# Block sums of w2 made mid-run and parked in DRAM, seven-product chunks from 9 to 15 with a plain last chunk, output rows together

## The chip, the cores and the metric

One core of a Trainium2 chip runs the whole program. The metric is the device time of one execution in microseconds (us). TensorE (PE) does the matmuls, VectorE (DVE), ScalarE (ACT) and GpSimd (POOL) the elementwise work; all DMAs are issued by SyncE (SP), in order, from one hardware queue.

## The reference

Attention over 8 batches and 8 heads of width 64: 512 local rows attend to the 65 nearest local rows and 32 global ones, 32 global rows attend to all. Its output x (8 x 544 x 512) goes through a two-dimensional Fourier transform and a feed-forward layer:

```python
X = np.fft.fft(x, axis=1)
X = np.fft.fft(X, axis=2)
u = x + np.real(X)
un = (u - mean(u)) / np.sqrt(var(u) + 1e-06)
return u + np.maximum(un @ w_ch1, 0.0) @ w_ch2     # w_ch1 512 x 2048, w_ch2 2048 x 512
```

The weights come as float64. All products keep float32 accuracy by splitting each factor into a float16 high and low part and summing three of the four partial products.

## The kernel before

**Stages.** The weights are loaded and split (names `w_...`). The attention runs over 32 head pairs (`load`, `scores`, `masked`, `exps`, `p_hi`, `p_lo`, `turn`, `values`, `norm`, and `g_...` for the global rows); `turn` is a DMA transpose. The Fourier stage of a batch (`d_...`) begins when its four pairs are done. The feed-forward layer (`l_...`, `f_...`) runs over 17 chunks of 256 rows: chunk 2b+k is half k of batch b, and chunk 16 holds the 32 rows that each batch has left over. So chunks, Fourier stages and attention of later batches overlap on the engines.

**A chunk.** For each of 8 pieces fp of the hidden width (256 columns), `f_first` (L1189) makes the first product in PSUM (`ps1`), `f_hi` (L1198, ACT) and `f_lo` (L1202, DVE) make the two halves of its ReLU, and `f_second` multiplies by w2. The plain form (L1211, chunks 0 to 9) is 2 x 6 matmuls of 512 columns for one fp. Chunks 10 to 16 (`c >= FAST`) use a seven-product (Strassen-Winograd) form, `f_fast` (L1263): 21 matmuls of 256 columns for one fp. It needs sums of the blocks of the ReLU (`f_relu` L1216 on ACT, `f_mix` L1221 to L1224 on DVE, `f_mhi` L1232 on ACT, `f_mlo` L1236 on POOL), and at the chunk's end `f_copy` and `f_join` (L1267 to L1279), before the residual `f_end` (L1284, DVE, one for each half j of 128 rows) and the store `f_out` (L1290; L1293 for chunk 16). During a chunk of that form the PSUM tile S (tag A) holds partial sums.

**The sums of w2.** That form also needs sums of the blocks of w2, hi and lo, one set `tw` for each fp: `t_sum` (L1150) adds hi and lo of the weights, `t_mix` (L1157 to L1160) makes four block sums, both on DVE, `t_hi` (L1171, ACT) and `t_lo` (L1176, DVE) split them. All operands lie in SBUF. The scratch tiles are those of the attention (`ph`, `pe`), and the sets are kept in its input buffers (`THOME`: qk, kT, vf, vN, vS). So the tasks wait for `done`: the last `scores` and `turn` and the last `g_turn`.

**The order.** `Plan.order` is a list scheduler that runs when the program is built: every task has an engine, an estimated duration, predecessors, buffers and a due time, and the plan fixes the order of each engine's instructions, SP's queue included. At the same time the task with the lower class goes first, then the earlier due time. The table `REL` gives earliest start times and `BIAS` shifts due times, by kind of task and stage. On the chip each engine then works through its list in that order, and waits wherever the next task's inputs aren't there.

The store of chunk 16 takes the rows to four batches for each half:

```python
for j in range(2):
    nc.sync.dma_start(self.out[4 * j:4 * j + 4, SL:T, :], u[:, j])
```

Of the kernel before, what the change touches and what calls it, by code (L numbers as in the profile page):

```python
# [32 lines left out]
FAST = 10  # L33
# [1575 lines left out]
```

## Time and profile before

| | us |
|---|---|
| median of 3 runs (1004.98, 1006.74, 1006.92) | 1006.74 |
| the profiled execution, its own time | 1002.04 |
| its span, first to last instruction | 1000.3 |
| PE busy | 890.2 |
| DVE busy | 654.8 |
| ACT busy | 614.5 |
| POOL busy | 630.3 |

The span's sum is made against the profiled execution; 1.74 us of its time lie outside the span, and the median of the runs is 4.70 us above it. Busy time is that of instructions on the engine, as the profile models their ends. A row of the timeline gives start, duration, engine, line and tile names, and in brackets the idle time ahead of it with what ended it.

### The profile page before, as it was taken

The page shows a single profiled execution, that of the slowest core. Times are in us where ns is not written, and L with a number is a line of the kernel's source. Part 1 is how long each engine was busy: PE and PEld are TensorE (multiplying, and loading weights), DVE is VectorE, ACT ScalarE, POOL GpSimd, SP SyncE. Part 2 cuts the span into 40 slices and gives each one's busy share as a digit, 9 for nine tenths or more (in the row PEclk, how much of TensorE's full clock was granted, in tenths as well). Part 3 has the DMA queues.
Part 4 walks back from the last instruction along what each step waited for, and adds up shares of the span by engine and source line. Part 5 has one row for each costly group of instructions (what it writes and reads, how often), then busy time and mean ns, then how long its engine had stood idle before and what let it go on. Part 6 is the DMA issues. An engine that isn't in the chain of part 4 may idle for free.

```text
span 1000.3 us, 31158 instructions
## 1 busy us (share of the span) xinstructions
PE 890.2 (89%) x12589; PEld 678.0 (68%) x12589; DVE 654.8 (65%) x1946; ACT 614.5 (61%) x1305; POOL 630.3 (63%) x905
## 2 busy tenths in 40 slices
PE   2652449999999999999999999996999999999993
PEld 1442337667676757667676766664889988888883
DVE  5987986257655676477556757599785755854442
ACT  6897788957786768697587766333443433443331
POOL 5599777796889688689959999217343432441211
PEclk8555559999999999999999999998999999999998
DMA  9998966558899667879779665620221311111000
GB/s 315 315 272 276 313 143 131 158 102 177 170 194 216 183 128 129 181 174 191 175 149 214 124 137 116 125 91 1 69 32 35 70 22 44 32 36 44 1 23 21
DMA packets 213785, 133.20 MB, mean 133 GB/s; under 512 B 165792, under 2 KB 183296, under 8 KB 213640
## 3 DMA queue, kind: packets, MB, share of 16 engines
q1 hardware_dynamic: 213640, 131.21, 56.0%
q8 instruction: 98, 1.61, 0.7%
q14 instruction: 47, 0.39, 0.1%
HBM read 64.98 MB, written 18.35 MB: 83 GB/s over the span
## 4 chain that ended last, share of the span: by engine, by line
PE 76%; DVE 11%; ACT 3%; DMA 3%; issue 2%; POOL 2%; SPq 1%; POOLq 0%; DVEq 0%; ACTq 0%
PE ps L1189 33%; PE acc L1211 19%; PE acc L1263 7%; PE S L1263 5%; PE bk L729 3%; PE S L681 2%; DVE tw L1176 1%; PE S L671 1%; PE bk L732 1%; DMA rw<-in_moe_w_ch 1%; DVE tf L1150 1%; DMA pl<-ph 1%; PE psd L1031 1%; PE S L764 1%; PE psd L998 1%
## 5 line engine op out<-in xcount | busy, mean ns | idle before, releaser
L1189 PE MATMUL ps<-uh,wh 128*128 128x256 f16 x3264 | 383.4, 274 | 0.7 <-DVE h L1202 0.7
L1189 PEld LDWEIGHTS <-wh 128*128 128x128 f16 x3264 | 315.4, 98 | 48.7 <-issue 1.5
L1211 PE MATMUL acc<-wh,h 128*128 128x512 f16 x960 | 224.4, 380 | 2.5 <-DVE h L1202 2.5
L1236 POOL TENSOR_TENSOR hs<-fz,hs 128x512 f16<-128x512 f32 x56 | 65.8, 1176 | 178.5 <-ACT hs L1232 132.4
L1211 PEld LDWEIGHTS <-h 128*128 128x128 f16 x960 | 88.7, 98 | 97.6 <-DVE h L1202 3.5
L1202 DVE SCALAR_TENSOR_TENSOR h<-ps,h 128x512 f16<-128x512 f32 x113 | 77.5, 686 | 58.6 <-ACT h L1198 58.2
L1198 ACT ACTIVATE h<-ps 128x512 f16<-128x512 f32 x113 | 66.9, 593 | 63.2 <-PE ps L1189 60.2
L1216 ACT ACTIVATE fx<-ps 128x512 f32<-128x512 f32 x56 | 33.4, 597 | 103.6 <-PE ps L1189 103.6
L700 ACT ACTIVATE pe<-pe,nm 128x160 f32<-128x160 f32 x256 | 87.8, 414 | 12.1 <-DVE nm L691 12.1
L707 POOL TENSOR_TENSOR ph<-pe,ph 128x512 f16<-128x512 f32 x64 | 76.7, 1198 | 28.3 <-ACT ph L703 27.5
L691 DVE CUSTOM_DVE_ANT_0 pe<-S,msk,z 128x160 f32<-128x160 f32 x192 | 62.2, 379 | 37.7 <-PE S L681 27.1
L1221 DVE TENSOR_TENSOR fz<-fx 128x128 f32<-128x128 f32 x56 | 20.5, 366 | 88.7 <-ACT fx L1216 87.5
L1263 PEld LDWEIGHTS <-hs 128*128 128x128 f16 x672 | 65.4, 98 | 8.5 <-POOL hs L1236 1.0
L1232 ACT ACTIVATE hs<-fz 128x512 f16<-128x512 f32 x56 | 35.3, 630 | 45.0 <-DVE fz L1224 43.5
L729 PEld LDWEIGHTS <-pl 128*64 128x64 f16 x1536 | 45.3, 117 | 23.1 <-issue 16.3
L729 PE MATMUL bk<-vN,pl 128*64 128x65 f16 x768 | 52.2, 203 | 8.5 <-DVE x L743 4.9
L621 POOL TENSOR_TENSOR vN<-vf,vN 128x640 f16<-128x640 f32 x32 | 43.3, 1356 | 14.0 <-ACT vN L617 10.6
L729 PE MATMUL bk<-vS,pl 128*64 128x65 f16 x768 | 51.7, 203 | 0.5 <-DMA vS<-vN 0.5
L732 PE MATMUL bk<-vN,pl 128*64 128x65 f16 x1024 | 48.9, 202 | 0.0
L703 ACT ACTIVATE ph<-pe 128x640 f16<-128x640 f32 x64 | 46.3, 726 | 1.8 <-DMA pl<-ph 1.0
L1263 PE MATMUL acc<-tw,hs 128*128 128x256 f16 x336 | 46.2, 273 | 0.4 <-POOL hs L1236 0.4
L506 POOL TENSOR_TENSOR wh<-wm,wh 128x512 f16<-128x512 f32 x32 | 36.9, 1159 | 11.9 <-ACT wm L499 10.5
(246 smaller groups left out, 1977.0 us busy)
## 6 DMA issues: line engine op xcount, KB each, us to landing
qk<-in_qk SPq DMA_DIRECT2D x32, 512.0 KB
vf<-in_v SPq DMA_DIRECT2D x32, 320.0 KB
raw<-in_moe_w_ch SPq DMA_DIRECT2D x17, 512.0 KB
vS<-vN SPq DMA_DIRECT2D x64, 130.0 KB
xs<-x SPq DMA_DIRECT2D x32, 256.0 KB
out<-u SPq DMA_DIRECT2D x16, 512.0 KB
x<-xs SPq DMA_DIRECT2D x24, 256.0 KB
u<-xs SPq DMA_DIRECT2D x24, 256.0 KB
```

Source lines behind the costliest of these rows:

```text
L691: nc.vector.tensor_tensor_reduce(self.per[(4 * p + j) % 4][:, h], S[:, h, 160 * n:160 * n + 160], self.msk[:, j], z[:, 8:9], 3e38, op0=ALU ...
L700: nc.scalar.activation(pe[:, h], pe[:, h], AF.Exp, bias=nm[:, n, h:h + 1], scale=-1.0)
L703: self.nc.scalar.activation(self.phr[i % 2][:, :, 96:256], self.pe2[i % 2], AF.Copy)
L707: self.nc.gpsimd.tensor_sub(ph[:, :, 256:384], pe[:, :, 32:160], ph[:, :, 128:256])
L729: nc.tensor.matmul(pv[r, n, h], pl[:, 3 * h + 1 + a, r], v, start=x == 0, stop=False)
L732: nc.tensor.matmul(pv[r, n, h], pl[:, 3 * h, r], vN[:, 4, c, h], start=False, stop=c == 1)
L1189: nc.tensor.matmul(ps[:, q], wt[:, w, c0:c0 + P], uh[:, :, 4 * a + kt, :], start=n == 0, stop=n == 11)
L1198: self.nc.scalar.activation(h[:, 0], self.fps[c, fp], AF.Relu)
L1202: self.nc.vector.scalar_tensor_tensor(h[:, 1], self.fps[c, fp], 0.0, h[:, 0], op0=ALU.max, op1=ALU.subtract)
L1211: nc.tensor.matmul(self.acc_f[c, j], h[:, a, q, j * P:(j + 1) * P], self.w[1, f][:, w, :], start=f == 0 and a == 0 and w == 0, stop=f == 1 ...
L1236: self.nc.gpsimd.tensor_sub(h[:, 1], self.fz.pop((c, fp)), h[:, 0])
L1263: nc.tensor.matmul(o, l[x], r[y], start=bool(first) and fp == 0 and n == 0, stop=bool(last) and fp == 7 and n == 2)
```

## The change

- `FAST, LAST = 9, 16` and `fast(c)`: the seven-product form is used for chunks 9 to 15. Chunk 16 is plain, without `f_copy` and `f_join`.
- The sums of w2 have scratch tiles of the Fourier stage (`x4` for the four sums, `eh` for the halves). They wait only for the weights, not for the attention; REL holds the unit of these tasks back to 235.6 in the plan's time. A new task `t_out` stores each set (512 KB) in a DRAM tile `td`, and `t_in` loads it into the place in SBUF where `t_hi` and `t_lo` put it before, after `done` (fp 4 to 7 also after the last `values` and `g_values`). The three sets with two places load by two DMAs: 8 stores, 11 loads.
- `f_hi` of chunk 9, all eight, and its first `f_relu` wait for `done`; its `f_second` for `t_in` of the same fp.
- The output tensor has 8 x 544 rows in the order in which the chunks make them, and the host puts them in place. Chunk 16 stores each half of 128 adjacent rows with a DMA of its own right after its `f_end` (`f_last`).
- The plan's estimates of the t tasks grow (1.2, 1.5, 1.2, 1.2 to 1.4, 1.9, 1.25, 1.6).
- `REL` and `BIAS` have other values. Apart from the loads of the weights, these are those of batches 2 and later, of chunks from 2 on, of the units T and f; attention and Fourier stages of batches 0 and 1 keep theirs.

```diff
-FAST = 10
+FAST, LAST = 9, 16
...
+def fast(c):
+    return FAST <= c < LAST
...
+        self.td = [dr.tile([P, 2, 2, 2, 256], F16, name=f"td{f}") for f in range(8)]
...
     def t_sum(self, fp):
-        f = self.cp.tile([P, 2, 512], F32, name="tf", tag="ph")
+        f = self.p1.tile([P, 4, 512], F32, name="tf", tag="x4")
...
+    def t_out(self, fp):
+        self.nc.sync.dma_start(self.td[fp], self.te.pop(fp))
+
+    def t_in(self, fp):
         home = THOME[fp]
         if len(home) == 2:
             t = [self.cp.tile([P, 2, 2, 256], F16, name="tw", tag=h) for h in home]
+            for i in range(2):
+                self.nc.sync.dma_start(t[i], self.td[fp][:, i])
         else:
             t = self.cp.tile([P, 2, 2, 2, 256], F16, name="tw", tag=home[0])
+            self.nc.sync.dma_start(t, self.td[fp])
...
     def f_out(self, c):
...
-        if b < B:
-            nc.sync.dma_start(self.out[b, 256 * k:256 * k + 256, :].rearrange("(j p) c -> p j c", j=2), u)
-        else:
-            for j in range(2):
-                nc.sync.dma_start(self.out[4 * j:4 * j + 4, SL:T, :], u[:, j])
+        self.nc.sync.dma_start(self.out[256 * c:256 * c + 256, :].rearrange("(j p) c -> p j c", j=2), self.u.pop(c))
+
+    def f_last(self, c, j):
+        self.nc.sync.dma_start(self.out[256 * c + P * j:256 * c + P * j + P, :], self.u[c][:, j])
...
-            add(("t_sum", fp), DVE, 1.2, self.t_sum, fp, after=done, seq=[("t_sum", fp - 1)] if fp else [], new=tf)
-            add(("t_mix", fp), DVE, 1.5, self.t_mix, fp, after=[("t_sum", fp)], seq=[("t_mix", fp - 1)] if fp else [], use=tf, new=tm)
...
+            add(("t_sum", fp), DVE, 1.4, self.t_sum, fp, after=[("w_lo", 16 + 2 * fp), ("w_lo", 17 + 2 * fp)], seq=[("t_sum", fp - 1)] if fp else [], new=[tf])
+            add(("t_mix", fp), DVE, 1.9, self.t_mix, fp, after=[("t_sum", fp)], use=[tf])
+            add(("t_hi", fp), ACT, 1.25, self.t_hi, fp, after=[("t_mix", fp)], seq=[("t_hi", fp - 1)] if fp else [], use=[tf], new=[te])
+            add(("t_lo", fp), DVE, 1.6, self.t_lo, fp, after=[("t_hi", fp)], use=[tf, te])
+            add(("t_out", fp), SP, .5, self.t_out, fp, after=[("t_lo", fp)], use=[te], kb=512)
+            add(("t_in", fp), SP, .6, self.t_in, fp, after=[("t_out", fp)] + done + ([("values", 63), ("g_values", 15)] if fp > 3 else []), seq=[("t_in", fp - 1)] if fp else [], new=tw, kb=512)
...
+            if c == 16:
+                for j in range(2):
+                    add(("f_last", c, j), SP, .6, self.f_last, c, j, after=[("f_end", c, j)], use=[u], kb=256, due=T + 20)
+                continue
...
-_OUT = (8, T, DM)
+_OUT = (8 * T, DM)
```

## Rows read from the trace of the kernel before

**Rows 1.** The page: the span, and the busy tenths of PE in 40 equal slices.

```profile
span 1000.3 us, 31158 instructions
...
PE   2652449999999999999999999996999999999993
```

**Rows 2.** Stretches: length, busy of PE, PEld, DVE, ACT, POOL (instructions), PE clock, DMA share, GB/s.

```profile
100.00:150.00 50.00, 23.17 (x341) 18.32 (x339) 44.79 (x118) 40.73 (x90) 38.83 (x61) 0.59 0.85 228
200.00:640.00 440.00, 437.82 (x7352) 305.38 (x7351) 276.85 (x934) 316.49 (x716) 361.15 (x537) 1.00 0.76 161
675.00:703.00 28.00, 19.20 (x150) 14.25 (x148) 27.77 (x34) 10.83 (x19) 18.36 (x18) 0.88 0.00 1
```

**Rows 3.** Waits of PE from 195 to 990 us: total, times, longest.

```profile
PE psd L998 <- DVE z L1020: 7.7, 1, 7.7
PE acc L1211 <- DVE h L1202: 2.5, 2, 2.2
...
PE ps L1189 <- DVE h L1202: 0.7, 1, 0.7
```

**Rows 4.** DVE, 674 to 688 us: start us, us, engine, line, operation, tiles, count.

```profile
674.05 5.87 DVE L1176 TENSOR_TENSOR tw<-tm,tw 128x512 f16<-128x512 f32 x2
...
687.07 0.46 DVE L1020 SCALAR_TENSOR_TENSOR z<-psd,z 128x274 f16<-128x274 f32 x1
```

**Rows 5.** Timeline of POOL, 674 us.

```profile
674.28 2.34 POOL L901 TENSOR_TENSOR s<-x 128x1020 f32<-128x1020 f32 x1
```

**Rows 6.** Timeline of PE, 648 to 706 us.

```profile
648.46 1.46 PE L1211 MATMUL acc<-wh,h 128*128 128x512 f16 x6
...
689.38 3.37 PE L1211 MATMUL acc<-wh,h 128*128 128x512 f16 x12
...
703.11 2.75 PE L1211 MATMUL acc<-wh,h 128*128 128x512 f16 x12
705.70 1.47 PE L1189 MATMUL ps<-uh,wh 128*128 128x256 f16 x12
```

**Rows 7.** Instructions on tile tw and tf: duration ns min/median/max, first and last start.

```profile
L1150 DVE TENSOR_TENSOR tf<-wh x16: 675/684/1207, 644.5 to 695.3; 128x512 f32<-128x512 f16 x16
L1157 DVE TENSOR_TENSOR tm<-tf x8: 415/420/947, 646.4 to 698.0; 128x256 f32<-128x256 f32 x8
...
L1176 DVE TENSOR_TENSOR tw<-tm,tw x16: 673/686/3119, 650.5 to 702.3; 128x512 f16<-128x512 f32 x16
```

**Rows 8.** Groups of DVE by line, 200 to 640 us: busy us, mean ns.

```profile
L1107 DVE TENSOR_TENSOR unh<-un,unh 128x512 f16<-128x512 f32 x18 | 15.2, 846 | 1.1 <-ACT unh L1103 1.1
```

**Rows 9.** Timeline of SP, the last transpose of the attention.

```profile
636.60 1.52 SPq L713 DMA_TRANSPOSE pl<-ph  x1
```

**Rows 10.** Timeline of all engines, 980 to 1000.3 us.

```profile
980.76 1.47 PE L1189 MATMUL ps<-uh,wh 128*128 128x256 f16 x12
...
982.83 0.59 ACT L1198 ACTIVATE hx<-ps 128x512 f16<-128x512 f32 x1
...
983.97 0.68 DVE L1202 SCALAR_TENSOR_TENSOR hx<-ps,hx 128x512 f16<-128x512 f32 x1
...
986.84 0.49 PE L1263 MATMUL S<-wh,hs 128*128 128x256 f16 x3
...
989.55 1.42 DVE L1284 SCALAR_TENSOR_TENSOR u<-fy,ve,u 128x512 f32<-128x512 f32 x2
990.33 1.27 SPq L1293 DMA_DIRECT2D out<-u  x2
```

**Rows 11.** DMA from 987 to 1000.3 us, 40 slices of 0.33 us, and packets.

```profile
GB/s 0 0 0 0 0 0 0 0 0 0 0 0 0 6 55 12 18 6 25 55 68 68 105 105 92 99 105 105 105 105 99 99 99 86 55 6 0 0 0 0
DMA packets 264, 0.52 MB, mean 39 GB/s; under 512 B 8, under 2 KB 8, under 8 KB 264
```

**Rows 12.** The same from 911 to 920 us, 40 slices of 0.225 us.

```profile
GB/s 0 0 0 0 0 0 0 0 0 0 0 0 0 0 0 246 400 400 355 410 391 128 0 0 0 73 0 0 0 0 0 0 0 0 0 0 0 0 0 0
DMA packets 273, 0.54 MB, mean 60 GB/s; under 512 B 16, under 2 KB 16, under 8 KB 272
```

More of the change, by code (lines that the diff above doesn't have):

```diff
@@ L1152, in t_mix, with t_lo @@
     def t_mix(self, fp):
-        ve, f = self.nc.vector, self.tf.pop(fp)
-        t = [self.cp.tile([P, 2, 256], F32, name="tm", tag=f"pe{i}") for i in range(2)]
-        self.tm[fp] = t
+        ve, f = self.nc.vector, self.tf[fp]
+        t = f[:, 2:4].rearrange("p a (b n) -> p (a b) n", b=2)
         (b11, b12), (b21, b22) = ((f[:, q, 0:256], f[:, q, 256:512]) for q in range(2))
-        ve.tensor_sub(t[0][:, 0], b12, b11)
-        ve.tensor_sub(t[0][:, 1], b22, t[0][:, 0])
-        ve.tensor_sub(t[1][:, 0], b22, b12)
-        ve.tensor_sub(t[1][:, 1], t[0][:, 1], b21)
+        ve.tensor_sub(t[:, 0], b12, b11)
+        ve.tensor_sub(t[:, 1], b22, t[:, 0])
+        ve.tensor_sub(t[:, 2], b22, b12)
+        ve.tensor_sub(t[:, 3], t[:, 1], b21)
     def t_hi(self, fp):
+        self.te[fp] = t = self.p1.tile([P, 2, 2, 2, 256], F16, name="te", tag="eh")
+        for i in range(2):
+            self.nc.scalar.activation(t[:, i, 0].rearrange("p a n -> p (a n)"), self.tf[fp][:, 2 + i], AF.Copy)
+    def t_lo(self, fp):
+        f, t = self.tf.pop(fp), self.te[fp]
+        for i in range(2):
+            self.nc.vector.tensor_sub(t[:, i, 1].rearrange("p a n -> p (a n)"), f[:, 2 + i], t[:, i, 0].rearrange("p a n -> p (a n)"))
+    def t_out(self, fp):
+        self.nc.sync.dma_start(self.td[fp], self.te.pop(fp))
+    def t_in(self, fp):
         home = THOME[fp]
@@ L1489, in run @@
             add(("d_rest", b), SP, 1.0, self.d_rest, b, after=[("d_addp", b, 2), ("d_addv", b, 2)], use=[("xfm", b)], kb=64, **kr)
+        done = [(n, i) for n in ("scores", "turn") for i in (62, 63)] + [("g_turn", 15)]
         for fp in range(8):
-            done = [(n, i) for n in ("scores", "turn") for i in (62, 63)] + [("g_turn", 15)]
-            tf, tm, tw = [("ph", "t", fp, x) for x in range(2)], [("per", "t", fp, x) for x in range(4)], [(h, "t", fp, x) for x, h in enumerate(TFREE[fp])]
-            add(("t_sum", fp), DVE, 1.2, self.t_sum, fp, after=done, seq=[("t_sum", fp - 1)] if fp else [], new=tf)
-            add(("t_mix", fp), DVE, 1.5, self.t_mix, fp, after=[("t_sum", fp)], seq=[("t_mix", fp - 1)] if fp else [], use=tf, new=tm)
-            add(("t_hi", fp), ACT, 1.2, self.t_hi, fp, after=[("t_mix", fp)] + ([("values", 63), ("g_values", 15)] if fp > 3 else []), seq=[("t_hi", fp - 1)] if fp else [], use=tm, new=tw)
-            add(("t_lo", fp), DVE, 1.2, self.t_lo, fp, after=[("t_hi", fp)], use=tm)
+            tf, te, tw = ("x4", "t", fp), ("eh", "t", fp), [(h, "t", fp, x) for x, h in enumerate(TFREE[fp])]
+            add(("t_sum", fp), DVE, 1.4, self.t_sum, fp, after=[("w_lo", 16 + 2 * fp), ("w_lo", 17 + 2 * fp)], seq=[("t_sum", fp - 1)] if fp else [], new=[tf])
[4 more added lines that the diff above has]
+            add(("t_in", fp), SP, .6, self.t_in, fp, after=[("t_out", fp)] + done + ([("values", 63), ("g_values", 15)] if fp > 3 else []), seq=[("t_in", fp - 1)] if fp else [], new=tw, kb=512)
         add(("l_load",), SP, .8, self.l_load, after=[("d_rest", b) for b in range(B)] + [("load_pair", 7, 1)], new=[("u", 16)], kb=512)
@@ L1528, in run @@
                         use=[uh] + ([ps] if q else []), new=[] if q else [ps], cls=8, due=T, alts=[["ps1"], ["bank"]] if c > FAST and q == 0 else None)
-                add(("f_hi", c, fp), ACT, .59, self.f_hi, c, fp, after=[("f_first", c, fp, 1)] + ([("t_mix", 7)] if c == FAST else []), use=[ps], new=[h], cls=1, due=T + 2.7, alts=[["h"], ["pgr"], ["pg"]] if c >= FAST else None)
+                add(("f_hi", c, fp), ACT, .59, self.f_hi, c, fp, after=[("f_first", c, fp, 1)] + (done if c == FAST else []), use=[ps], new=[h], cls=1, due=T + 2.7, alts=[["h"], ["pgr"], ["pg"]] if c >= FAST else None)
                 add(("f_lo", c, fp), DVE, .69, self.f_lo, c, fp, after=[("f_hi", c, fp)], use=[ps, h], cls=1, due=T + 3.5)
-                if c >= FAST:
+                if fast(c):
                     hx, hz, hs = ("qT", "f", c, fp), [("per", "f", c, fp, x) for x in range(2)], ("pl", "f", c, fp)
-                    add(("f_relu", c, fp), ACT, .59, self.f_relu, c, fp, after=[("f_first", c, fp, 1)] + ([("t_mix", 7)] if c == FAST and fp == 0 else []) + ([("f_relu", c, fp - 1)] if fp else []), use=[ps], new=[hx], cls=1, due=T + 2.7)
-                    add(("f_mix", c, fp), DVE, .9, self.f_mix, c, fp, after=[("f_relu", c, fp)], seq=[("f_mix", c, fp - 1)] if fp else [("f_mix", c - 1, 7)] if c > FAST else [("t_mix", 7)], use=[hx], new=hz, cls=1, due=T + 3.5)
+                    add(("f_relu", c, fp), ACT, .59, self.f_relu, c, fp, after=[("f_first", c, fp, 1)] + (done if c == FAST and fp == 0 else []) + ([("f_relu", c, fp - 1)] if fp else []), use=[ps], new=[hx], cls=1, due=T + 2.7)
+                    add(("f_mix", c, fp), DVE, .9, self.f_mix, c, fp, after=[("f_relu", c, fp)], seq=[("f_mix", c, fp - 1)] if fp else [("f_mix", c - 1, 7)] if c > FAST else [], use=[hx], new=hz, cls=1, due=T + 3.5)
                     add(("f_mhi", c, fp), ACT, .6, self.f_mhi, c, fp, after=[("f_mix", c, fp)], use=hz, new=[hs], cls=1, due=T + 4.3, alts=[["pl"], ["plg"], ["x"]])
@@ L1539, in run @@
                         prv = [("f_second", c, fp - 1, j)] if fp else []
-                        add(("f_second", c, fp, j), PE, 1.29 if j else .97, self.f_fast, c, fp, j, after=[("f_mlo", c, fp) if j else ("f_lo", c, fp)] + ([("t_lo", fp)] if c == FAST else []) + ([("f_second", c, fp, 0)] if j else []) + prv,
+                        add(("f_second", c, fp, j), PE, 1.29 if j else .97, self.f_fast, c, fp, j, after=[("f_mlo", c, fp) if j else ("f_lo", c, fp)] + ([("t_in", fp)] if c == FAST else []) + ([("f_second", c, fp, 0)] if j else []) + prv,
                             use=([hs, ("A", "f", c)] if j else [h]) + ([h] if j else [hs]) + (accs[j] if fp else []), new=[] if fp else accs[j], cls=7, due=T + 5)
@@ L1547, in run @@
                     add(("f_second", c, fp, j), PE, 1.3, self.f_second, c, fp, j, after=[("f_lo", c, fp)] + w2 + prv, use=[h] + ([acc] if fp else []), new=[] if fp else [acc], cls=7, due=T + 5)
[L1548 removed]
+            if fast(c):
                 fy = [("ph", "f", c, x) for x in range(2)]
                 accs = [("acc0", "f", c), ("acc1", "f", c), ("A", "f", c)]
[L1551 removed]
+                add(("f_copy", c), ACT, .45, self.f_copy, c, after=[("f_second", c, 7, 0)], seq=[("f_copy", c - 1)] if c > FAST else [], use=accs[:1], new=fy, cls=1, due=T + 10)
                 add(("f_join", c), DVE, 3.0, self.f_join, c, after=[("f_second", c, 7, 1), ("f_copy", c)], use=accs + fy, cls=1, due=T + 10)
             for j in range(2):
[L1554 removed]
+                add(("f_end", c, j), DVE, .75, self.f_end, c, j, after=[("f_second", c, 7, j), ("l_root", c)] + ([("f_join", c)] if fast(c) else []), use=(fy if fast(c) else [(f"acc{j}", "f", c)]) + [u, ve], cls=1, due=T + 10)
+            if c == 16:
+                for j in range(2):
+                    add(("f_last", c, j), SP, .6, self.f_last, c, j, after=[("f_end", c, j)], use=[u], kb=256, due=T + 20)
+                continue
             add(("f_out", c), SP, .6, self.f_out, c, after=[("f_end", c, 0), ("f_end", c, 1)], use=[u], kb=512, due=T + 20)
```

24 lines of the change are left out of this document (7 added, 17 removed).

## The prediction, made before the changed kernel ran

> **What bounds the kernel now.** I read the page first, for where PE isn't full: 9 in nearly every slice from the eighth on, a 6 near 690 us, a 3 at the end [rows 1]. The stretches then give sizes: PE is busy 437.82 of 440 us from 200 to 640, and 19.20 of 28 us from 675 to 703 [rows 2]. So the middle is bound by PE, with 2.18 us idle, and work taken off another engine there gains nothing. The hole at 690 is 8.80 us. The waits of PE say what ends it: 7.7 us on one tile z of the Fourier stage and small ones on `f_lo`, all made by DVE [rows 3]. The timeline shows why: two `t_lo` ran from 674.05 for 5.87 us, more t tasks after them, and z came only at 687.07 [rows 4]. DVE is busy 27.77 of those 28 us [rows 2], and the chain of waits follows DVE there: the sums of w2 hold it up. The last view is the end: PE's last products start at 986.84, but the span ends at 1000.3 [rows 1, 10].
>
> **The t tasks leave 645 to 702.** Of the hole I count all 8.80 us as gone, and what PE lost at the lower clock behind it: twelve matmuls took 3.37 us after the hole and 2.75 us later [rows 6], 0.62. That is -9.4 us. The rest of the old t stretch gives nothing, as PE was fed there. What is late next is the new chunk 9: its second products need `done` and the parked sets. The last `turn` is issued at 636.60 for 1.52 us, so `done` comes near 639 to 640, and the first second product of chunk 9 ran at 648.46 before [rows 6, 9]. About 10 us of cover for a load of 0.5 MB, which takes 7 slices of 0.225 us, 1.6 us, at full rate [rows 12]. The eleven loads take some 13 us of the queue, and each fp of a chunk lasts about 5 us, so later loads stay ahead: I cost them at nothing as long as `done` isn't later than now. If it is, each us beyond 10 is a us of PE.
>
> **The t tasks arrive mid-run.** One fp is two sums, four mixes and two lows: 2 x 0.684 + 4 x 0.420 + 2 x 0.686 = 4.42 us of DVE, and 35.4 us for eight [rows 7]. DVE has 440 - 276.85 = 163 us idle from 200 to 640 [rows 2], and ACT's sixteen more conversions have 123 us. As throughput this fits. It isn't free, because a DVE task that comes late makes PE wait in its fixed order; the row for that is the 2.5 us which PE waited for `f_lo` in the present load [rows 3]. The t tasks will also be longer than their medians: beside POOL's 2.34 us subtraction two `t_lo` took 5.87 instead of 1.37 us [rows 4, 5, 7], and `l_lo`, the same kind of instruction, averages 846 ns in the middle against 686 [rows 7, 8]. By the latter the eight sets are 44 us, DVE's load goes from 63% to 73%, and I take 3 us of PE, somewhat more than the stall seen. The ends are 0, when the plan's slack covers it, and 25, worked out under the slow rival.
>
> The stores t_out: eight issues on SP's queue, each behind a `t_lo`, with the loads and transposes of the attention behind them. Their bytes are 8 x 1.6 = 13 us of DMA against 24% of 440 us that is free [rows 2]. I put their waits into the same 3 us. The scratch tiles x4 and eh are those of the Fourier stage, so a Fourier stage may start some us later; cover for that is chunks made from batches long finished.
>
> The Trainium skill bears on this (SBUF — State Buffer, Who interferes with whom): a VectorE instruction with two operands in SBUF and a GpSimd instruction that reads SBUF exclude each other, and whichever starts second waits for the whole of the first. By that rule POOL pays for every t instruction that starts first, and where all of them did, the sum would be that of the slow rival below, 5 us slower, instead of -16.9. The trace agrees for DVE's side (5.87 us for two); no row shows what POOL lost.
>
> **Chunks 9 and 16.** The seven-product form saves 12 x 512 - 21 x 256 = 768 columns for an fp. At 2.59 us for the 12 x 512 (703.11 to 705.70 [rows 6]) that is 0.32, or 2.6 us for a chunk. Chunk 9 gains it and chunk 16 loses it: 0. The sums that chunk 9 adds on DVE, ACT and POOL lie in a stretch that loses the t tasks, and are covered as in chunks 10 to 15.
>
> **The end.** Before: the last first product ends at 982.23, the last second product at 987.33 [rows 10], 5.10 us. Plain: `f_hi` 0.59, then `f_lo` 0.68, now without `f_relu` and `f_mix` ahead of them, with two gaps of 0.1 that is 1.47 us; then ten of the twelve matmuls are left (two need only the high half), 2.16 us. Sum 3.63, or -1.5 us; the ends are 0 and -2, by the order in which the plan puts the last pieces.
>
> From PE's end to the span's end it was 1000.3 - 987.33 = 12.97 us, with `f_join` and two `f_end`. Now one half `f_end`, 1.42/2 = 0.71, then the issue. The first bytes came 1.0 us after the issue at 990.33 (slice 14 starts at 991.3) and the span ended 1.3 us after the last ones (slice 36 ends at 999.0) [rows 10, 11]. The old stores crept at about 100 GB/s with 8 small packets for two DMAs, where a usual store has 16 for one and moves at 400 [rows 11, 12]: I read that as 4 engines against 16. Half the bytes of rows 12 is 0.8 us. With 0.2 for two hand-overs: 0.2 + 0.71 + 1.0 + 0.8 + 1.3 = 4.0, or -9.0 us. If the new store crept as well, 256 KB at 100 GB/s is 2.6 us, and the term -7.2. I take -9.0, as the new store has 128 rows like the usual ones.
>
> **The plan's tables.** Loads of weights get other start times, and so all that follows is ordered anew. From 100 to 150 us PE is busy 23.17 of 50 us [rows 2], so up to 27 us could be won there or as much lost; which needed weights come late I can't read from a table. The first pieces' loads and batches 0 and 1 keep their times. I take 0, and 5 us either way for the range.
>
> **Sum.** -9.4 + 3 + 0 - 1.5 - 9.0 + 0 = -16.9 us. Against the profiled execution that is 1002.04 - 16.9 = 985.1; against the median of the runs, which lies 4.70 above it, 1006.74 - 16.9 = 989.8. I forecast the latter.
>
> **The rivals.** *The hole moves* (0.20). `done` or the last parked sets come late, or t tasks stay so long that they meet the end of the attention, and PE stands where it stood before. For: DVE's and SP's lists are full just before 640, and chunk 9 was the cover. Against: 10 us of slack now. The gain of 9.4 is lost and the end's 10.5 stays: 1006.74 - 10.5 + 3 = 999.2.
>
> *The attention is slowed, and the kernel with it* (0.09): the one that ends slower. POOL is busy 361.15 of 440 us [rows 2] and sits in every link of the attention's chain. If each of the 35.4 us of t work holds POOL off, it comes to 397 of 440, and if that all goes to the chain, `done` is 35.4 us later, 25 beyond the cover; then PE waits 25 us in front of chunk 9 instead of 3: -16.9 - 3 + 25 = 5 us slower, 1012. It decides at about 20 us of wait. Against it: POOL still has idle time, PE's own work paces the middle, and only part of the t work can meet a POOL instruction.
>
> *The new order costs the start* (0.07): PE finds late weights from 100 to 150 us, by 14 us, half of what the idle time there allows; 1004.
>
> **Chances.** The forecast has 0.64. A measurement of this kernel can't tell about 0.2%, 2 us, from no change. Faster: 0.64 + 0.16 of the first rival + 0.04 of the third = 0.84; same: 0.04 + 0.02 = 0.06; slower: 0.09 + 0.01 = 0.10. The range goes from 982 (mid-run free, the start 5 better) to 1001, which takes in the first rival and leaves out the slow one and most of the third.
>
> **What would show it.** No wait of PE over 2 us from 640 to 710 and DVE below 90% there; t instructions after 200 us at 0.42 to 0.9 us each; PE still over 435 of 440 us from 200 to 640; the last store with 16 small packets and about 4 us from PE's end to the span's end. It is wrong if PE's waits mid-run exceed 8 us, if chunk 9's first f_second waits for tw or `turn`, or if the first product of chunk 0 starts much later.

## The result, and the profile after

The changed kernel takes 991.22 us (median of 990.96, 991.47, 992.10 and 990.40), beside 1005.86 us for the kernel before: a ratio of 0.9857 [0.9837, 0.9877]. The forecast was 989.8 us. The profiled execution took 990.96 us, with a span of 989.2.

The page, span and PE in 40 slices [rows 1]. The 6 near 690 us is gone, and so is the 3 at the end.

```profile
span 989.2 us, 31139 instructions
...
PE   2552449999999999999999999999999999999998
```

The stretches, with the columns of [rows 2]. First the kernel before, two stretches that weren't shown:

```profile
640.00:700.00 60.00, 51.90 (x550) 36.65 (x548) 56.70 (x101) 21.06 (x40) 22.69 (x22) 0.94 0.22 56
700.00:750.00 50.00, 49.11 (x443) 42.41 (x441) 40.01 (x103) 21.10 (x39) 18.90 (x35) 1.00 0.24 49
```

Then the changed kernel:

```profile
100.00:150.00 50.00, 22.07 (x311) 16.77 (x307) 44.50 (x118) 39.89 (x88) 40.10 (x62) 0.58 0.86 229
...
200.00:640.00 440.00, 433.99 (x7219) 300.30 (x7218) 317.20 (x952) 318.46 (x720) 362.12 (x515) 1.00 0.76 170
640.00:700.00 60.00, 57.72 (x640) 48.30 (x638) 42.19 (x107) 24.30 (x46) 31.73 (x50) 1.00 0.42 125
675.00:703.00 28.00, 25.71 (x248) 22.33 (x246) 25.42 (x59) 12.03 (x23) 19.93 (x26) 1.00 0.13 25
700.00:750.00 50.00, 47.82 (x452) 42.38 (x450) 40.44 (x94) 22.21 (x41) 25.80 (x38) 1.00 0.15 44
```

DVE took the t tasks into the middle: 276.85 us busy before, 317.20 now. PE is idle there 6.01 us instead of 2.18. From 640 to 700 PE is idle 2.28 us instead of 8.10, and at full clock. From 700 to 750 it is idle 2.18 us instead of 0.89, so not all of the hole is gone. The waits of PE from 195 to 990 us [rows 3] have many small entries where one large one stood:

```profile
PE acc L1224 <- DVE h L1215: 2.4, 2, 1.5
PE acc L1276 <- DVE hx L1215: 1.8, 1, 1.8
PE acc L1276 <- DVE h L1215: 1.7, 1, 1.7
PE bk L734 <- issue: 1.5, 1, 1.5
```

The second and third end at 684 and 711 us. The timelines of DVE, POOL and PE of the changed kernel, in this order, show what stood before them [rows 4, 5, 6]:

```profile
679.50 0.81 DVE L1234 TENSOR_TENSOR fz<-fx 128x128 f32<-128x128 f32 x1
680.34 2.32 DVE L1235 TENSOR_TENSOR fz<-fz,fx 128x128 f32<-128x128 f32 x1
682.58 0.28 DVE L1236 TENSOR_TENSOR fz<-fx 128x128 f32<-128x128 f32 x1
682.78 0.28 DVE L1237 TENSOR_TENSOR fz<-fx,fz 128x128 f32<-128x128 f32 x1
682.99 0.68 DVE L1215 SCALAR_TENSOR_TENSOR hx<-ps,hx 128x512 f16<-128x512 f32 x1
...
704.87 3.28 DVE L1297 SCALAR_TENSOR_TENSOR u<-fy,ve,u 128x512 f32<-128x512 f32 x2
...
680.12 2.40 POOL L906 TENSOR_TENSOR s<-x 128x1020 f32<-128x1020 f32 x1
...
683.72 0.61 PE L1276 MATMUL acc<-wh,hx 128*128 128x256 f16 x4 [1.83 <-DVE hx L1215]
...
710.67 0.61 PE L1276 MATMUL acc<-wh,h 128*128 128x256 f16 x4 [1.72 <-DVE h L1215]
```

One instruction of `f_mix` (L1235), whose median is 0.29 us, lasts 2.32 us, to 682.66: POOL's subtraction of the Fourier stage ends at 682.52. `f_lo` stands behind it and PE behind that. At 704.87 it is the two `f_end` of chunk 9: 3.28 us instead of 1.42 [rows 10]. The old hole began with two `t_lo` beside the same subtraction [rows 4, 5]. So it looks like the same mechanism at its old place, with smaller instructions in it. No run takes POOL's instruction away: that it is what holds DVE up is read from the timeline.

Two rows of before and two of after say why these instructions meet now. Before, the first `f_mix` (chunk 10) came 9.6 us after POOL's last sum of Fourier inputs; now the first (chunk 9) comes at 651.84, and POOL's sums go on to 717.5 us (the short `d_addp`, which come later in both, are left aside):

```profile
693.00 0.90 POOL L939 TENSOR_TENSOR s<-s 128x256 f32<-128x256 f32 x1
703.54 0.27 DVE L1221 TENSOR_TENSOR fz<-fx 128x128 f32<-128x128 f32 x1
...
651.84 0.29 DVE L1234 TENSOR_TENSOR fz<-fx 128x128 f32<-128x128 f32 x1 [0.78 <-ACT fx L1229]
717.04 0.45 POOL L972 TENSOR_TENSOR et<-st 32x128 f32<-32x128 f32 x1
```

The t instructions themselves, on tile tf, with the columns of [rows 7]:

```profile
L1155 DVE TENSOR_TENSOR tf<-wh x16: 677/726/1639, 224.0 to 548.7; 128x512 f32<-128x512 f16 x16
...
L1174 DVE TENSOR_TENSOR te<-tf,te x16: 674/912/1729, 272.3 to 561.6; 128x512 f16<-128x512 f32 x16
L1161 DVE TENSOR_TENSOR tf<-tf x8: 418/696/1059, 228.0 to 551.8; 128x256 f32<-128x256 f32 x8
...
L1164 DVE TENSOR_TENSOR tf<-tf x8: 409/790/2844, 230.5 to 553.9; 128x256 f32<-128x256 f32 x8
```

They are spread from 224 to 562 us and keep DVE busy for 57.4 us, against 35.4 by their old medians. The parked sets are loaded from 636.4 to 660.3 us, and PE waits for none of them.

The end, timeline of all engines and the DMA's 40 slices (0.43 us each) from 972 us [rows 10, 11]:

```profile
980.04 5.34 PE L1224 MATMUL acc<-wh,h 128*128 128x512 f16 x24
...
984.12 0.75 DVE L1297 SCALAR_TENSOR_TENSOR u<-acc,ve,u 128x512 f32<-128x512 f32 x1 [2.56 <-PE acc L1224]
984.90 1.64 SPq L1303 DMA_DIRECT2D out<-u  x2
985.42 0.75 DVE L1297 SCALAR_TENSOR_TENSOR u<-acc,ve,u 128x512 f32<-128x512 f32 x1 [0.54 <-PE acc L1224]
```

```profile
GB/s 0 0 0 0 0 0 0 0 0 0 0 0 0 0 0 0 0 0 0 0 0 0 0 0 0 0 0 0 0 0 0 10 381 219 10 381 219 0 0 0
DMA packets 288, 0.52 MB, mean 30 GB/s; under 512 B 32, under 2 KB 32, under 8 KB 288
```

PE works without a pause up to 985.38, and the span ends 3.82 us later (12.97 before). The two stores have 32 small packets (under 512 B) instead of 8 and move at up to 381 GB/s instead of some 100.

Put together from the first `f_first` on (at 143.46 us before, at 145.10 after), the spans differ by 12.7 us:

| stretch | us | predicted |
|---|---|---|
| 150 to 200, PE idle | +0.7 | 0 |
| 200 to 640, PE idle 2.18 to 6.01 | +3.8 | +3 |
| 640 to 750, PE idle 8.99 to 4.46, and 1.5 of slow clock behind the old hole | -6.0 | -9.4 |
| before PE's end, its idle time 2.29 to 0 | -2.3 | -1.5 |
| from PE's end to the span's end | -9.15 | -9.0 |

The five lines make -12.95. The clock's 1.5 us come from the granted clock before, behind 7.7 us of idle PE: it is 0.50 from 687.5 to 690 us, the lower of the two levels (1.2 GHz), and 0.70 on the mean from 690 to 691.

### The profile page after: what moved, and what is told of

The parts are those of the page before. It is cut to its first block, busy times and chain, and to the rows that moved or that the text cites. A ratio compares the mean times of both kernels' runs of the same rounds, so it can differ in the third digit from the quotient of the medians.

```text
span 989.2 us, 31139 instructions
## 1 busy us (share of the span) xinstructions
PE 889.9 (90%) x12589; PEld 677.9 (69%) x12589; DVE 670.2 (68%) x1946; ACT 611.6 (62%) x1305; POOL 635.9 (64%) x905
## 4 chain that ended last, share of the span: by engine, by line
PE 71%; DVE 10%; POOL 6%; DMA 4%; ACT 3%; issue 3%; SPq 1%; DVEq 0%; POOLq 0%; ACTq 0%
PE ps L1202 31%; PE acc L1224 18%; PE acc L1276 7%; PE S L1276 5%; PE bk L734 2%; DMA pl<-ph 2%; PE S L686 1%; PE bk L737 1%; DVE pe L696 1%; PE psd L1036 1%; PE S L676 1%; PE psd L1003 1%; DMA vf<-in_v 1%; PE S L769 1%; POOL vN L626 1%
## 5 line engine op out<-in xcount | busy, mean ns | idle before, releaser
L1224 PE MATMUL acc<-wh,h 128*128 128x512 f16 x924 | 214.7, 379 | 2.5 <-DVE h L1215 2.4
L1224 PEld LDWEIGHTS <-h 128*128 128x128 f16 x924 | 85.1, 98 | 95.5 <-DVE h L1215 4.3
L1215 DVE SCALAR_TENSOR_TENSOR h<-ps,h 128x512 f16<-128x512 f32 x110 | 75.3, 684 | 56.7 <-ACT h L1211 55.4
```

Source lines behind the costliest of these rows:

```text
L1215: self.nc.vector.scalar_tensor_tensor(h[:, 1], self.fps[c, fp], 0.0, h[:, 0], op0=ALU.max, op1=ALU.subtract)
L1224: nc.tensor.matmul(self.acc_f[c, j], h[:, a, q, j * P:(j + 1) * P], self.w[1, f][:, w, :], start=f == 0 and a == 0 and w == 0, stop=f == 1 ...
```

## The experiments

Ratios are to the kernel before, run beside on the same chip (its medians were 1004.14, 1005.35 and 1004.37 us in the three sets). My theory after the result: the end is worth some 9 us, the hole's place is a collision of DVE's two-input instructions with POOL's Fourier work, and the t work mid-run is nearly free. The rivals: the t work costs PE mid-run in proportion to its length; the gain is due to the new tables.

**The end alone.** The kernel before, with a plain chunk 16, a store for each half and rows in the new order. Chunk 9 stays plain too, so one chunk fewer has the seven-product form.

```diff
-FAST = 10
+FAST, LAST = 10, 16
...
+    def f_last(self, c, j):
+        self.nc.sync.dma_start(self.out[256 * c + P * j:256 * c + P * j + P, :], self.u[c][:, j])
```

> The kernel before with only the end changed: chunk 16 plain, its two halves stored by DMAs of their own into adjacent rows; sums of w2 and tables as before, seven products for chunks 10 to 15. Theory (the terms add up): the two traces give 9.1 us less from PE's end to the span's end and 2.3 us less idle PE ahead of it, and one seven-product chunk fewer costs 2.6: 8.8 us faster than before, ratio about 0.991. Rival (the end's gain hangs on the new plan): within 3 us of before, ratio 0.997 or more.

Measured: 996.77 us, 0.9929 [0.9914, 0.9945], or -7.4 us. The tail is 3.9 us (PE ends at 990.74, the span at 994.6), and the hole is where it was (7.8 us on z). The end is the larger part of the gain. Though the edit gives the plan another list of tasks, DVE, ACT and POOL do their instructions in the order of before up to chunk 16.

**All but the end.** The changed kernel with the seven-product form also for chunk 16, and the old store.

```diff
-FAST, LAST = 9, 16
+FAST, LAST = 9, 17
...
-        self.nc.sync.dma_start(self.out[256 * c:256 * c + 256, :].rearrange("(j p) c -> p j c", j=2), self.u.pop(c))
+            for j in range(2):
+                nc.sync.dma_start(self.out[4 * j:4 * j + 4, SL:T, :], u[:, j])
```

> The changed kernel without its end: chunk 16 in seven products with its join, and its rows stored as before into four batches for each half; sums mid-run and parked, chunk 9 in seven products. Theory: the hole's 7 us less the 4 us mid-run less, in both traces' rows, some 3 us for the start, plus 2.6 for one seven-product chunk more than before: 3 to 6 us faster than before, ratio 0.994 to 0.997. Rival (the move of the sums is worth the predicted 6.4 us and the 2.6 on top): 9 us faster, ratio 0.991.

Measured: 1001.28 us, 0.9968 [0.9958, 0.9979], -2.9 us. It has one seven-product chunk more than before, 2.6 us by the prediction's count. So moving the sums of w2 and chunk 9 brought little. The two parts sum to -10.3 us, where the whole change gives -14.6. The gap of 4.3 us is more than the noise of the three results taken together, some 2.8. In the traces, from the first `f_first` on, it is 4.0 us. Of that 0.8 is idle PE just before its end in the first run, where the changed kernel has none, 1.0 is more idle PE mid-run in this one (7.04 us against 6.01), and some 1.7 come from a granted clock of 0.57 from 384 to 388 us here, behind a wait of 1.7 us. The order of the engines is that of the changed kernel up to chunk 16, so the last two are differences between executions.

**The old row places.** The changed kernel, but each half's store goes to four batches again.

```diff
-        self.nc.sync.dma_start(self.out[256 * c + P * j:256 * c + P * j + P, :], self.u[c][:, j])
+        self.nc.sync.dma_start(self.out[4 * j:4 * j + 4, SL:T, :], self.u[c][:, j])
```

> The changed kernel with the old place of the output rows alone: each half of chunk 16 still has its own DMA after its f_end, but goes to 32 rows in each of four batches. Theory (four DMA engines carry it instead of sixteen): 256 KB at about 100 GB/s take 2.6 us instead of 0.7, so the end is 1.9 us longer, ratio to before about 0.988 instead of 0.986, 8 small packets for the two stores instead of 32. Rival (the slow store of before came from two big stores at once or from the far-apart rows): the packets number 32 and the end stays within 0.5 us of the changed kernel's 3.8 us.

Measured: 995.32 us, 0.9915 [0.9897, 0.9932]. PE ends at 984.48, the span at 993.7: 9.2 us, 5.4 longer than with rows together, where I had reckoned with the creep of one half. The DMA from 982 us, slices of 0.29 us:

```profile
DMA  0000000000025050023122222222222222100000
GB/s 0 0 0 0 0 0 0 0 0 0 0 49 35 0 21 7 28 56 70 49 105 105 98 98 112 91 105 112 91 105 112 91 105 84 42 21 0 0 0 0
DMA packets 264, 0.52 MB, mean 45 GB/s; under 512 B 8, under 2 KB 8, under 8 KB 264
```

Eight small packets for two DMAs, and with both in flight (issued from 984.00 to 985.87) the rate stays at 91 to 112 GB/s. The row DMA, the busy share of the 16 engines in tenths, stands at 2 there, where the changed kernel's stores reach 9. That fits four busy engines for both stores together, and so the same four for each; the trace doesn't name them. The Trainium skill (DMA: Bandwidth & Descriptors, Why a DMA increments its semaphore by 16 and not by 1) says that the number of engines is the largest up to 16 that divides the slowest dimension of both sides, and that they are the lowest-numbered ones. Four batches as the outer dimension give 4 by that, 128 rows give 16. The packets agree with both numbers, 4 and 16 for a DMA; which engines they are no run here shows.

**Four stores for a half.** The same row places, but a DMA for each batch, of 32 rows and 64 KB.

```diff
+        for i in range(4):
+            self.nc.sync.dma_start(self.out[4 * j + i, SL:T, :], self.u[c][32 * i:32 * i + 32, j])
```

> The changed kernel with the old place of the output rows, and four DMAs of 32 rows for each half instead of one DMA of four pieces. Theory (what made the old store slow is that one DMA of four pieces runs on four engines): 16 small packets for each DMA, 128 in all, transfers at several hundred GB/s, and the end, with four issues of 0.4 to 0.6 us after the last f_end, about 5.5 us long, ratio to before about 0.987. Rival (rows far apart in DRAM are slow): about 100 GB/s again and an end of 9 us.

Measured: 995.34 us, 0.9903 [0.9879, 0.9926]; the profiled execution took 991.15, the other three 994.6 to 996.3. In the profile PE ends at 983.80 and the span at 989.3: a tail of 5.5 us, as expected. The DMA from 972 us, slices of 0.43 us:

```profile
GB/s 0 0 0 0 0 0 0 0 0 0 0 0 0 0 0 0 0 0 0 0 0 0 0 0 0 0 0 0 152 147 147 142 142 137 119 133 95 0 0 0
DMA packets 384, 0.52 MB, mean 30 GB/s; under 512 B 128, under 2 KB 128, under 8 KB 384
```

Now each DMA has 16 small packets, and the rate is still only about 145 GB/s. The eight issues take SP 3.62 us, 0.45 us each, and 64 KB in 0.45 us is 145 GB/s: so the issuing seems to pace the store. The median is 4.6 us above the changed kernel by the ratios, and the longer tail explains 1.7; what the timed runs lost besides, the one profile doesn't show. By the ratios of the runs the four stores aren't clearly faster than the one (0.9903 and 0.9915, with intervals that overlap), so their gain of 3.7 us at the end is shown by the profiles alone.

**The kernel before without the sums.** The order is that of before; DVE's t instructions are left out, and `t_hi` copies the weights instead, so the output isn't that of the reference.

```diff
-            self.nc.vector.tensor_add(f[:, q], w[:, 0], w[:, 1])
...
-        ve.tensor_sub(t[0][:, 0], b12, b11)
...
-            self.nc.vector.tensor_sub(self.wt[fp][i][:, 1], tm[i], self.wt[fp][i][:, 0])
```

> The kernel before in its own order, without the sums of w2: no DVE instruction of t_sum, t_mix and t_lo, and t_hi copies the weights themselves on ACT, so the second products of chunks 10 to 16 have other factors. Theory (the sums on DVE, held up by POOL, made the hole): PE idles under 1.5 us from 640 to 700 instead of 8.1, 8 to 10 us faster than before, ratio about 0.991. Rival (the Fourier stage of that stretch holds PE up by itself): 5 us or more of idle PE stay there, ratio over 0.995.

Measured: 993.87 us, 0.9900 [0.9875, 0.9924], or -10.5 us. Stretches:

```profile
640.00:700.00 60.00, 60.00 (x628) 43.41 (x627) 25.82 (x61) 31.06 (x48) 21.38 (x24) 1.00 0.26 68
700.00:750.00 50.00, 49.80 (x463) 44.33 (x461) 31.15 (x84) 19.03 (x35) 19.21 (x36) 1.00 0.23 54
```

The hole was the sums' doing, all of it: 60.00 of 60 us. The prediction's -9.4 was nearly the right price for taking them away from there. But with chunk 9 plain, as here, there are no `f_mix` in its place.

**The changed kernel without the sums.** The same edit there, with the order unchanged.

> The changed kernel in the same order, without the sums of w2: no DVE instruction of t_sum, t_mix and t_lo is given, t_hi copies the weights themselves on ACT (1 us each instead of 0.6), so the second products of chunks 9 to 15 have other factors. Theory (the sums cost PE 3 to 4 us by coming late): PE's idle time from 200 to 640 falls from 4 to 6 us to about 2, 2 to 4 us faster than the changed kernel, ratio 0.982 to 0.984. Rival (the idle time is the new order's own): unchanged within 1 us.

Measured: 988.59 us, 0.9834 [0.9810, 0.9858]; by the ratios 2.3 us less than the changed kernel. Stretches:

```profile
200.00:640.00 440.00, 436.97 (x7342) 304.03 (x7340) 263.97 (x894) 326.54 (x724) 354.33 (x519) 1.00 0.78 173
640.00:700.00 60.00, 57.72 (x563) 48.62 (x558) 42.16 (x109) 24.66 (x47) 30.58 (x47) 1.00 0.36 99
```

From 200 to 640 PE has 3.03 us idle instead of 6.01. But 6.01 is one execution. Up to chunk 9 the run without the end, both runs with other stores and the one with the low half first (below) keep the changed kernel's order on DVE, ACT and POOL, and have the t work; their idle time there is 7.04, 3.01, 5.35 and 6.23 us. The first and the second of the stores:

```profile
200.00:640.00 440.00, 436.99 (x7245) 303.05 (x7243) 316.75 (x953) 321.00 (x724) 365.63 (x524) 1.00 0.78 172
200.00:640.00 440.00, 434.65 (x7230) 301.51 (x7228) 319.37 (x951) 318.19 (x720) 363.55 (x514) 1.00 0.78 171
```

What PE waits for tells more than the sum. Its waits for DVE in this stretch add up to 4.1 us in the changed kernel, to 4.1, 0.5, 2.8 and 3.6 in these four, and to nothing in the one profile without the sums. So the t work costs PE between 0.5 and 4 us mid-run, 3 on the mean; the 2.3 us by the ratios are within their noise (some 3.1). From 640 to 700 nothing changes: 57.72 here, as in the changed kernel. So the rest of the hole isn't owed to the sums any more.

**Chunk 9 plain.**

```diff
-FAST, LAST = 9, 16
+FAST, LAST = 10, 16
```

> The changed kernel with chunk 9 in plain form (FAST = 10; the tables, the sums and the end as changed). Theory (products go by columns, 768 for each fp, while the plan holds): 2.6 us slower than the changed kernel, ratio to before about 0.988. Rival (a plain chunk 9 covers the end of the attention and the loads of the parked sets): as fast as the changed kernel or faster, ratio 0.986 or less, with less idle PE than 4.5 us from 680 to 750.

Measured: 999.43 us, 0.9932 [0.9906, 0.9959], 7.5 us above the changed kernel by the ratios and not the 2 to 3 of the lost form. From 640 to 700 PE is busy 59.88 us, in line with chunk 9's own `f_mix` and `f_end` as what is late there; but from 200 to 640 only 429.29. The one-line edit gave the plan another list of tasks, and from some 470 us on all three engines have another order, so it isn't a clean test of chunk 9.

**The low half first.** For chunks 9 and 10 `f_hi` goes a class ahead of `f_relu`, so that `f_lo` doesn't stand behind the mixes.

```diff
-                add(("f_hi", c, fp), ACT, .59, self.f_hi, c, fp, after=[("f_first", c, fp, 1)] + (done if c == FAST else []), use=[ps], new=[h], cls=1,
+                add(("f_hi", c, fp), ACT, .59, self.f_hi, c, fp, after=[("f_first", c, fp, 1)] + (done if c == FAST else []), use=[ps], new=[h], cls=0 if c in (FAST, FAST + 1) else 1,
...
```

> The changed kernel with f_hi of chunks 9 and 10 a class ahead of f_relu, so that f_lo needn't stand behind f_mix on DVE while POOL still does Fourier stages. Theory (the two new waits of 1.8 and 1.7 us on f_lo come from f_mix and f_end being held up ahead of it): both shrink under 0.5 us, 2 to 3 us faster than the changed kernel, ratio to before about 0.983. Rival (the second halves' factors, which f_mix begins, come late instead, since their chain over four instructions is the longer one): the waits move to POOL's hs, the time stays within 1.5 us of the changed kernel or is longer.

Measured: 995.28 us, 0.9905 [0.9886, 0.9923]: no gain, some 5 us lost. Its waits of PE include

```profile
PE ps L1202 <- DVE h L1215: 2.9, 2, 2.1
PE S L1276 <- DVE zr L1025: 1.8, 1, 1.8
PE acc L1276 <- DVE hx L1215: 1.4, 1, 1.4
```

The waits are handed round among the same tasks (PE idle 6.43 us from 640 to 750, 4.46 in the changed kernel). What I tried to mend is the order; the collision with POOL stays.

**The sums twice.** Every t instruction of DVE issued twice, in the same order of tasks.

```diff
+        for _ in range(2):
...
+            ve.tensor_sub(t[:, 0], b12, b11)
```

> The changed kernel in the same order, with each DVE instruction of the t tasks given twice (64 more, the values unchanged). Theory (DVE has room, only lateness costs): 57 us more on DVE from 200 to 640, some 375 of 440 busy, PE's idle time there from 4 to 6 us to 8 to 12, 3 to 6 us slower than the changed kernel. Rival (the attention is slowed through POOL and DVE): PE idle over 20 us, 15 us or more slower, ratio to before 1.0 or more.

Measured: 1021.51 us, 1.0162 [1.0138, 1.0186]. My theory fell. Stretch and the first two waits of PE:

```profile
200.00:640.00 440.00, 415.04 (x6677) 284.07 (x6676) 338.26 (x966) 305.65 (x690) 343.87 (x491) 0.98 0.71 159
```

```profile
PE S L676 <- DVE nm L696: 11.1, 4, 5.3
PE acc L1227 <- DVE h L1218: 6.6, 3, 3.4
```

The t work went from 57 to 100 us, and PE idled 25.0 us from 200 to 640 instead of 6.0, with DVE busy 338 of 440. The first 57 us had cost PE some 3 us; the next 42 cost it 19 us of idle time and the kernel about 30 us. Of the rest 8.6 us are longer busy time of PE, most of it in this stretch at a granted clock of 0.98 instead of 1.00. The late task is now the masking of the attention's scores (nm): the work is no longer hidden by the slack of the order but delays the attention's chain. This is the place of the slow rival.

**The old tables.** The changed kernel with REL and BIAS of before and only the unit T held back to 235.6.

```diff
-REL = {('w_load', 3): 11.8, ('w_load', 4): 25.1, ('w_load', 9): 22.9,
...
+REL = {('w_load', 2): 7.2, ('w_load', 4): 7.1, ('w_load', 10): 43.3,
...
```

> The changed kernel with the tables REL and BIAS of the kernel before (and the one entry that holds the t tasks back to 235.6). Theory (the tables are worth little): within 5 us of the changed kernel, ratio to before 0.981 to 0.991, PE idle at most 10 us from 200 to 640. Rival (the new order carries the gain of the move): a hole of 8 us or more comes back near the end of the attention, ratio 0.993 or more.

Measured: 1025.28 us, 1.0207 [1.0190, 1.0224], far outside. The loss isn't at the end of the attention, as the rival had it: PE is busy 60.00 us from 640 to 700. From 200 to 640 it is busy 410.38 of 440 us, and in its largest wait the scores' product stands behind the Fourier stage's assembly (asm) on DVE. The t tasks are packed into 226 to 382 us there, so either their crowding or the order of the rest could be the cause.

**The old tables without the sums** (the edits of the last one and of the one without sums together) tells these apart.

> The same omission of the sums in the changed kernel with the old tables, which had 29.6 us of idle PE from 200 to 640 and a ratio of 1.021. First theory (the t tasks, which that plan packs between 233 and 382 us, come late and hold up the attention): idle PE falls under 10 us, ratio 1.0 or less. Second theory (the order itself, with what the longer list of tasks moved, leaves PE idle): idle PE stays over 20 us, ratio 1.01 or more.

Measured: 1023.85 us, 1.0181 [1.0162, 1.0200]. Stretch and largest wait, of the old tables first, then of the old tables without sums:

```profile
200.00:640.00 440.00, 410.38 (x6799) 285.52 (x6798) 295.47 (x924) 304.22 (x690) 336.51 (x490) 0.96 0.71 159
```

```profile
PE S L676 <- DVE asm L1053: 14.2, 2, 9.6
```

```profile
200.00:640.00 440.00, 413.55 (x6893) 287.84 (x6892) 254.07 (x864) 311.99 (x695) 328.80 (x492) 0.96 0.71 160
```

```profile
PE S L676 <- DVE asm L1053: 13.5, 2, 9.3
```

DVE has 41 us less to do, and PE is still idle 26.5 us instead of 29.6. It is the order that costs, not the load: made from the new list of tasks with the old tables, it has the scores' product wait for the Fourier stage. Why the plan puts them so I didn't follow.

**The new tables alone.** The kernel before with REL and BIAS of after.

```diff
-REL = {('w_load', 2): 7.2, ('w_load', 4): 7.1, ('w_load', 10): 43.3,
...
+REL = {('w_load', 3): 11.8, ('w_load', 4): 25.1, ('w_load', 9): 22.9,
...
```

> The kernel before with the REL and BIAS of the changed kernel, nothing else. Theory (a table fits one list of tasks, and the tables hold none of the gain): PE idles 10 us or more from 200 to 640, ratio 1.005 or more. Rival (the new tables are better whatever the tasks): idle PE of at most 5 us there, ratio 1.0 or less.

Measured: 1009.90 us, 1.0056 [1.0038, 1.0074]. So the tables aren't better by themselves, and the rival that they alone make the gain is out. The theory's ratio held, but not its reason: PE idles 4.37 us from 200 to 640 and not 10. That each set fits its own list of tasks is shown strongly one way only, by the 34 us of the old tables with the new list; the new tables with the old list cost 0.6%.

No version that computes the reference beat the changed kernel.

## Why the prediction was right, and where not

**The end was right, its first part by another way.** -1.5 and -9.0 were forecast, -2.3 and -9.15 measured. The -1.5 was worked out as a shorter way from the last first product to PE's end, 3.63 us instead of 5.10. That way is 5.2 us in the changed kernel (980.20 to 985.38). The gain, which also lies past the stated end of -2, came because the plan left 24 matmuls for it and PE had no pause. The tail came out as read: a small `f_end` of 0.75 us, first bytes about a microsecond after the issue, 16 small packets for a store at 381 GB/s. "4 engines against 16" was read from 8 and 16 small packets [rows 11, 12], and the old row places brought back both the packets and the creep. Its fallback, -7.2 "if the new store crept as well", was mis-sized: creeping costs 5.4 us more and not 1.8, as both halves together move at the 100 GB/s that it took for one.

**The hole's term was the one mis-sized.** "Of the hole I count all 8.80 us as gone" was wrong: -9.4 was taken, -6.0 measured (the clock's part was 1.5 and not 0.62, so the idle part fell shorter still). The step that failed is under the chunks: "the sums that chunk 9 adds on DVE, ACT and POOL lie in a stretch that loses the t tasks, and are covered as in chunks 10 to 15". The cover that chunks 10 to 15 had before was that POOL's sums of the Fourier stage had ended, 9.6 us before the first `f_mix`; now they run to 717.5 us, beside chunk 9. The run without the sums in the kernel before shows that -10.5 was there to be had. The run without them in the changed kernel shows the 2.28 us standing after the t work is gone, and the timeline shows chunk 9's `f_mix` and `f_end` in the place of the old `t_lo`, beside POOL's same subtraction. The two waits stand with 1.8 and 1.7 us in every run that keeps this order, also in the one without the sums. So the first rival, "the hole moves", came in part: not by late `done` or late sets, as it was argued, but by the same collision with other instructions.

**The t work mid-run.** +3 was taken, +3.8 measured in the two profiles, and waits of 0.5 to 4 us for DVE in five executions, 3 on the mean. The size was right as far as these tell. Its working was not: 44 us of DVE were counted by one neighbour's stretch, [rows 8], and it was 57.4. The upper end of 25 was no idle caution. With 100 us of t work PE idled 25.0 us, so the slow rival's place is real, and the change sits some 40 us of DVE work from it. But its price doesn't grow in a line, and it came through DVE's list (nm, `f_lo`) rather than through POOL, which was busy 343.87 us there against 362.12.

**Who pays for the exclusion.** The t work on DVE is 22 us longer than its clean 35.4. POOL's busy time from 200 to 640 is 362.12, against 354.33 us in the run without the sums, 7.8 more, by one profile of each: its scaling of vf, for instance, takes 947 ns against 793. The Trainium skill (SBUF — State Buffer, Who interferes with whom) has whichever starts second wait. The trace agrees that both sides pay; here DVE paid about three times as much. The sum in which POOL pays for all 35.4 us isn't what happened.

**The tables** were taken as 0, with 5 us either way for the start. For the start that holds: PE is busy 22.07 us from 100 to 150 (23.17 before). As a reason it fell short. The tables carry the middle: with the old ones the same tasks take 34 us more. The change's new tables are what keeps its order from that. The 0 was right for the change as it came; that it hung on the new tables the prediction didn't see.

**The base.** The forecast is 1.4 us off, but its terms were less exact than that: -16.9 against -12.7 by the two traces. The profiled execution of before was an early one. Its first `f_first` is at 143.46, and in other executions of the kernels here, with the start's loads the same or nearly so, it lies between 143.85 and 147.8. The forecast added the 4.70 us by which the median lay above that execution, and for the changed kernel this distance is 0.26 us (990.96 to 991.22). Measured against each other the medians differ by 14.6 us, by which the terms were 2.3 too large. Against the profiled executions alone (1002.04 to 990.96) they were 5.8 too large, and the added distance was 4.4 too long: that the forecast lies within 1.4 us is in part luck.

**The signs named.** No wait over 2 us from 640 to 710: held, 1.83 the longest. DVE below 90% there: held for 640 to 700, 70%, though from 675 to 703 it is 91%. t instructions at 0.42 to 0.9 us: the medians are 0.70 to 0.94, the longest 2.84. PE over 435 us from 200 to 640: just missed, 433.99, though 436.99 in the run with the old row places. The store and the tail: held. None of the three signs of being wrong came.

## What to carry to other kernels

Where work is taken out of a hole, ask which instruction stands there next, and whether it has the same form: here the collision of DVE's two-input instructions with POOL's long one outlived the tasks that had shown it. Hidden work has a margin as well as a price; double it once and measure, since the first 57 us cost PE some 3 us and the next 42 cost it 19. An idle time of a few us in one profile isn't yet a price: look at several executions of the same order, and at what the waits are for. An order fitted to one list of tasks is part of the kernel: an experiment that adds or drops tasks can change the order, so keep the list and empty the tasks instead.

## What the hardware showed that I had not expected

- Two stores with four pieces each moved at 91 to 112 GB/s with both in flight and the 16 engines busy to 0.2; with 16 small packets for each, the tail was 5.4 us shorter.
- Eight DMAs of 64 KB, each with 16 small packets, moved at 145 GB/s, which is 64 KB for each of SP's issues of 0.45 us, where two of 256 KB reach 381.
- One DVE instruction of 0.29 us lasted 2.32 us beside one POOL instruction of 2.40 us, and ended 0.14 us after it. A pair of `f_end` went from 1.42 to 3.28 us beside a row of POOL instructions of 0.7 to 1.3 us.
